# Attention in transposed score tiles: 96 queries by 128 keys, no row maximum, denominators from a ones column

## The chip, the cores and the metric

The kernel runs on one core of a Trainium2 chip. The metric is the device time of one execution in microseconds (us). Five engines work side by side, each through its own instructions in order: PE multiplies matrices (its weight loads are shown as PEld and overlap the multiplications), DVE and ACT do element-wise work, POOL does the same more slowly and can issue transfers, and SP only issues transfers (DMA). A measurement of this kernel can tell about 0.5% from no change.

## What is computed

The input is float32; the two channel weights come as float64 words. Attention over a local window and block summaries is followed by a Fourier mix and a two-layer channel block:

```python
batch, n_heads, seq, head_dim = (4, 8, 768, 64)
block, window = (32, 16)
k_sum = k.reshape(B, H, nb, block, D).max(axis=3)
v_sum = v.reshape(B, H, nb, block, D).mean(axis=3)
scores_l = scale * np.matmul(q, k.transpose(0, 1, 3, 2))
mask_l = np.abs(pos[:, None] - pos[None, :]) < window
scores_s = scale * np.einsum('bhsd,bhnd->bhsn', q, k_sum)
scores_s = scores_s + np.log(block)
...
scores_all = scores_all - np.max(scores_all, axis=-1, keepdims=True)
a = np.exp(scores_all)
a = a / (np.sum(a, axis=-1, keepdims=True) + 1e-09)
...
X = np.fft.fft(x, axis=1)
X = np.fft.fft(X, axis=2)
mixed = np.real(X).astype(np.float32)
u = x + mixed
...
un = (u - mu) / np.sqrt(var + 1e-06)
ch = np.maximum(un @ w_ch1, 0.0) @ w_ch2
return (u + ch).astype(np.float32)
```

Every query sees 31 keys around it and 24 summaries (the maximum of each block of 32 keys, the mean of its values). The exponentials are divided by their sum.

## The kernel before

The program has five stages. In stage b (0 to 3) the attention of batch b is woven with other work: in stage 0 with the conversion of the channel weights (gen_weights, lines 266 to 290), in stages 1 to 3 with the Fourier mix and the channel layers of the batch before (gen_post, from line 301). Stage 4 holds gen_post of the last batch alone. The weaving is written as generators: drive (line 406) takes one step of the attention, then two of gen_post (one of gen_weights), and so on. A scheduler then orders each engine's instructions from this order and their dependences, so work can move ahead of its place in the code.

gen_attention goes through four pairs of heads per batch, three steps per pair, each step on two tiles of 128 queries. The names that the rows use are these.

- prepare: keys and queries are transposed on PE (qk, line 153) and copied by ACT. DVE takes the block maxima (line 158). PE averages the values of the blocks (vm, line 166, 6 matmuls), and DVE copies the averages (line 170).
- scores: queries stand in the output's rows. PE computes 192 columns for each tile and head (sc, lines 183, 185, 186): 128 own keys, 32 edge keys, 24 summaries, padding. A head has 64 channels, so the first head's operands lie in rows 0 to 63 and the second's in rows 64 to 127. DVE adds the mask (line 187), takes the row maximum (lines 192, 193), ACT takes the exponential with the row sum (line 196), DVE takes the reciprocal (lines 199, 200).
- turn: PE transposes the probabilities (pt, line 209, 6 per step); DVE and ACT copy them (line 211).
- values: PE multiplies them with edge values and summaries (av, line 220) and with the own values (line 223); DVE multiplies by the reciprocal and writes x (line 224).

gen_post folds x on DVE (sd, zw, fg, lines 311 to 321), transforms it on PE (y, lines 327 and 331; mx, lines 344 and 345), normalises it, transposes it (unt, line 365), and runs the channel layers (hp, line 373; ch, line 384), whose results DVE and ACT take out. It ends with the stores of x. gen_post(b) needs the whole of x of batch b.

A float32 matmul stands in the trace as two instructions, here called passes; a transpose is one. SP issues the loads of keys and queries, the weight loads (raw, line 277) and the stores; POOL issues the loads of values and edge values.

## Time and profile before

| | |
|---|---|
| time of three runs, us | 1127.8, 1131.44, 1132.7 (median 1131.44) |
| the profiled execution's span, first to last instruction, us | 1126.7 |
| what lies around the span (median less span), us | 4.7 |
| PE busy in the span | 1031.1 us (92%) |
| DVE busy in the span | 439.4 us (39%) |
| ACT, POOL busy | 228.8 us (20%), 122.9 us (11%) |

The time of the profiled execution itself is not recorded apart from its span; the median stands for it. The span falls into the stages at the first y instruction of each batch: 163.5, 417.4, 673.8 and 920.8 us. An engine's share of the whole span mixes stages with different limits, so the shares are read stage by stage.

### The profile page before, as it was taken

What the parts mean: (1) busy time and instruction counts of PE and PEld (TensorE: products, weight loads), DVE (VectorE), ACT (ScalarE), POOL (GpSimd) and SP (SyncE); (2) the same over time, 40 slices, a digit from 0 to 9 for tenths busy, and PEclk for the clock granted to TensorE, in tenths of its full rate; (3) what the DMA queues carried; (4) which work ended last, traced back from release to release, by engine and by line L of the source; (5) the groups of instructions that cost most, each with busy time, mean ns of one, the idle gap of its engine ahead of it and who ended that gap; (6) DMA issues with size and microseconds to landing.
All of it is one profiled execution on the core that took longest, in us unless ns stands there. A gap on an engine that the chain in (4) does not pass through costs nothing. (4 is left out here: it accounts for less than half of the span.)

```text
span 1126.7 us, 10580 instructions
## 1 busy us (share of the span) xinstructions
PE 1031.1 (92%) x4144; PEld 656.7 (58%) x4144; DVE 439.4 (39%) x906; ACT 228.8 (20%) x668; POOL 122.9 (11%) x164
## 2 busy tenths in 40 slices
PE   5376689999998989999999989999999978999998
PEld 4365568664565457764566457765566546544543
DVE  4999988421332047521322037522222046101000
ACT  2456533310121002311112003311112001000100
POOL 2556520100101010100101010100100000000000
PEclk8655679999998989999999999999999989999999
DMA  9585411100202011010202011000000000000000
GB/s 265 154 220 165 138 48 29 45 1 9 64 1 45 10 35 29 17 29 9 64 1 46 10 36 29 18 1 9 27 10 1 18 11 1 1 9 19 1 9 19
DMA packets 63106, 46.59 MB, mean 41 GB/s; under 512 B 52688, under 2 KB 53968, under 8 KB 62928
## 3 DMA queue, kind: packets, MB, share of 16 engines
q1 hardware_dynamic: 58528, 37.63, 12.2%
q0 software_dynamic: 4096, 7.61, 2.5%
q10 hardware_dynamic: 432, 0.67, 0.2%
q8 instruction: 33, 0.54, 0.2%
q14 instruction: 17, 0.14, 0.0%
HBM read 39.60 MB, written 6.29 MB: 41 GB/s over the span
## 5 line engine op out<-in xcount | busy, mean ns | idle before, releaser
L373 PE MATMUL hp<-unT,w 128*128 128x384 f32 x1024 | 345.1, 493 | 3.1 <-DVE unT L366 3.1
L384 PE MATMUL ch<-w,h 128*128 128x512 f32 x768 | 337.5, 594 | 0.0
L373 PEld LDWEIGHTS hp<-unT,w 128*128 128x128 f32 x1024 | 193.0, 193 | 129.9 <-issue 4.3
L384 PEld LDWEIGHTS ch<-w,h 128*128 128x128 f32 x768 | 143.4, 191 | 165.8 <-issue 163.8
L196 ACT ACTIVATE s<-s,mx 128x192 f32<-128x192 f32 x192 | 85.1, 444 | 238.8 <-DVE mx L193 237.6
L376 DVE TENSOR_SCALAR h<-hp 128x384 f32<-128x384 f32 x64 | 35.7, 558 | 209.2 <-PE hp L373 203.6
L299 DVE TENSOR_TENSOR x<-ch,x 128x512 f32<-128x512 f32 x24 | 16.6, 692 | 181.8 <-PE ch L384 181.8
L378 ACT ACTIVATE h<-hp 128x384 f32<-128x384 f32 x64 | 31.2, 487 | 273.4 <-PE hp L373 273.4
L209 PE MATMUL pt<-ident,s 128*128 128x128 f32 x288 | 50.8, 303 | 23.6 <-DVE ve L170 6.8
L143 POOL DMA_DIRECT2D ve<-in_v_dram x32 | 17.7, 553 | 496.9 <-PE av L220 496.9
L187 DVE SCALAR_TENSOR_TENSOR s<-sc,mask 128x384 f32<-128x384 f32 x96 | 50.4, 550 | 36.0 <-PE sc L183 32.7
L223 PE MATMUL av<-vn,ptT 128*128 128x64 f32 x384 | 61.2, 288 | 0.0
L209 PEld LDWEIGHTS pt<-ident,s 128*128 128x128 f32 x288 | 36.4, 153 | 40.7 <-issue 15.1
L223 PEld LDWEIGHTS av<-vn,ptT 128*128 128x128 f32 x384 | 59.2, 220 | 0.1
L327 PE MATMUL y<-fs,fg 128*128 128x193 f32 x192 | 45.2, 389 | 14.1 <-DVE fg L318 14.1
L220 PE MATMUL av<-ve,ptT 128*128 128x128 f32 x192 | 46.5, 328 | 11.9 <-DVE x L224 11.7
L183 PE MATMUL sc<-kw,qt 64*128 64x192 f32 x192 | 49.3, 381 | 8.5 <-DVE s L187 8.5
L289 POOL TENSOR_TENSOR w<-w,cvt 128x512 f32<-128x512 f32 x32 | 51.4, 1618 | 35.6 <-DVE w L287 35.6
L211 ACT COPY ptT<-pt 128x384 f32<-128x384 f32 x48 | 22.7, 472 | 152.6 <-PE pt L209 152.6
L224 DVE TENSOR_TENSOR x<-av,rcp 128x256 f32<-128x256 f32 x48 | 20.2, 421 | 79.2 <-PE av L223 79.0
L220 PEld LDWEIGHTS av<-ve,ptT 128*128 128x128 f32 x192 | 35.7, 219 | 25.1 <-DVE x L224 15.3
L327 PEld LDWEIGHTS y<-fs,fg 128*128 128x128 f32 x192 | 38.5, 230 | 18.3 <-DVE fg L318 8.5
(70 smaller groups left out, 974.9 us busy)
## 6 DMA issues: line engine op xcount, KB each, us to landing
raw<-in_moe_w_ch_dram SPq DMA_DIRECT2D x32, 512.0 KB, 4.1
kn<-in_k_dram SPq DMA_DIRECT2D x32, 192.0 KB, 4.0
vn<-in_v_dram POOLq DMA_DIRECT2D x32, 192.0 KB, 3.9
qn<-in_q_dram SPq DMA_DIRECT2D x32, 192.0 KB, 4.6
out_dram<-x SPq DMA_DIRECT2D x24, 256.0 KB, 2.0
ve<-in_v_dram POOLq DMA_DIRECT2D x64, 20.0 KB, 2.7
fs<-c_fs SPq DMA_DIRECT2D x1, 1158.0 KB, 8.6
fd<-c_fd SPq DMA_DIRECT2D x1, 768.0 KB, 8.7
```

What stands on the lines that cost most here:

```text
L183: nc.tensor.matmul(ps[:, j, :], qt[rows, t, :], kw[rows, t, :], start=True, stop=True)
L187: nc.vector.scalar_tensor_tensor(out=s[:, :, e, :], in0=ps, scalar=1.0 / float(np.sqrt(D)), in1=mask[:, sp:sp + 2, 0:KW] if e else mask[:, ...
L196: nc.scalar.activation(out=a, in_=a, func=AF.Exp, bias=mx[:, i:i + 1], scale=1.0, accum_out=den[:, i:i + 1])
L209: nc.tensor.transpose(ps[:, i, :], sv[:, c:c + P], ident)
L220: nc.tensor.matmul(ps[:, j].rearrange("p e d -> p (e d)"), pts[j][:, 2, :], ve[:, t, :], start=True, stop=False)
L223: nc.tensor.matmul(ps[:, j, e, :], pts[j][:, e, :], vn[:, t, e, :], start=False, stop=(e == 1))
L289: nc.gpsimd.tensor_tensor(out=dst, in0=dst, in1=tmp[:, 0, :], op=ALU.mult)
L327: nc.tensor.matmul(y, fg[:, st, P * g:P * (g + 1)], fs[:, g % 2, par, st, :], start=(st == 0), stop=(st == HT - 1))
L373: nc.tensor.matmul(ps, w1[:, d, P * n:P * (n + 1)], unT[:, d, :], start=(d == 0), stop=(d == NDT - 1))
L376: nc.vector.tensor_scalar(out=hT[n], in0=ps, scalar1=0.0, scalar2=None, op0=ALU.max)
L378: nc.scalar.activation(out=hT[n], in_=ps, func=AF.Relu)
L384: nc.tensor.matmul(ps, hT[n][:, P * i:P * (i + 1)], w2[:, n, :], start=(n == 0), stop=(n == NIT - 1))
```

## The change

The attention of the kernel is written anew, and the old kernel stands behind it as a second program that runs only if a flag is set. gen_weights and gen_post are the same text.

- Queries come in 96s, and keys stand in the rows of the score tile: 128 keys cover 96 queries with 16 keys on each side. Per pair there are 16 score matmuls of 96 columns (8 windows, two heads), and 2 more of 384 columns for all summaries.
- There is no mask to add, no row maximum and no transpose of the probabilities. ACT takes the exponential straight from the scores, DVE multiplies by a 0/1 band (128x768, twice per pair), and the result is already the left operand of the product with the values.
- The values carry a column of ones (65 columns for 64), so the product gives the denominators. The summaries' ones column holds 32 and their values are block sums, which takes the place of log(32) and the mean. 16 matmuls of 65 columns and 8 of 130 per pair.
- Block sums come from a load of their own (vb) and a DVE reduction, then go by DMA to where they are needed (vs). The outputs (xs) have 96 rows and go by six DMAs per pair to x, which has 128.
- All transfers but three constants are issued by SP.
- PSUM is divided into four single buffers and two of two banks.
- The reciprocals of all denominators are kept (rec). After batch 3's attention they are tested against 2^-40 and 2^40; a flag is read by all engines at the end, and a branch goes round the old program if it is 0.

The diff, cut to its core (the removed lines are the functions printed above):

```diff
+QT = 96
+LIM = 2.0 ** 40
...
+    def two_banks(name):
+        return psum.tile([P, 2, 512], FP, tag="two", bufs=2, name=name)
+
+    def one_bank(shape, name):
+        return psum.tile(shape, FP, tag="one", bufs=4, name=name)
...
+    def block_sums(b, gg):
+
+        raw = apool.tile([4 * nb, BLOCK, D], FP, tag="vb", bufs=1, name=f"vb_{b}_{gg}")
+        nc.sync.dma_start(out=raw.rearrange("p f d -> p (f d)"),
+                          in_=v[b, 4 * gg:4 * gg + 4].rearrange("h (n f) d -> (h n) (f d)", f=BLOCK))
+        vb = spool.tile([4 * nb, D], FP, tag="vbs", bufs=2, name=f"vbs_{b}_{gg}")
+        nc.vector.tensor_reduce(out=vb, in_=raw.rearrange("p f d -> p d f"), op=ALU.add, axis=AX.X)
+        sums[b, gg] = vb
+
+    def load_values(b, g):
+        vw, vs = vw_bufs[g % 2], vs_bufs[g % 2]
+        if g % 2 == 0:
+            block_sums(b, g // 2)
+        for e in range(2):
+            src = v[b, 2 * g + e].rearrange("(t p) d -> p t d", p=QT)
+            nc.sync.dma_start(out=vw[W:W + QT, :, e, 0:D], in_=src)
+            nc.sync.dma_start(out=vw[0:W, 1:NQ, e, 0:D], in_=src[QT - W:QT, 0:NQ - 1, :])
+            nc.sync.dma_start(out=vw[W + QT:P, 0:NQ - 1, e, 0:D], in_=src[0:W, 1:NQ, :])
+            i = 2 * (g % 2) + e
+            for c in range(2):
+                r = 64 * c + 32 * e
+                nc.sync.dma_start(out=vs[r:r + nb, e, 0:D], in_=sums[b, g // 2][nb * i:nb * (i + 1), :])
...
+    def scores(b, g, r):
+        kt, qt = kt_bufs[g % 2], nat[b, g]
+        ps = two_banks(f"sc_{b}_{g}_{r}")
+        for i, (h, j) in enumerate(windows(r)):
+            o = QT * (4 * h + j)
+            for e in range(2):
+                rows = slice(D * e, D * (e + 1))
+                nc.tensor.matmul(ps[:, e, QT * i:QT * (i + 1)], kt[rows, o:o + P], qt[rows, o:o + QT],
+                                 start=True, stop=True)
+        p = apool.tile([P, 2, 4, QT], FP, tag="p", bufs=2, name=f"p_{b}_{g}_{r}")
+        nc.scalar.activation(out=p.rearrange("p e i c -> p e (i c)"), in_=ps[:, :, 0:4 * QT], func=AF.Exp, scale=SC)
+        pv = p.rearrange("p e i c -> p (e i) c")
+        nc.vector.tensor_tensor(out=pv, in0=pv, in1=band[:, None, :].to_broadcast([P, 8, QT]), op=ALU.mult)
+        return p
+
+    def sum_scores(b, g):
+        km, qt = km_bufs[g % 2], nat[b, g]
+        ps = one_bank([P, S2], f"ss_{b}_{g}")
+        for h in range(2):
+            nc.tensor.matmul(ps[64 * h:64 * (h + 1), :], km.rearrange("p e n -> p (e n)"),
+                             qt[:, S2 * h:S2 * (h + 1)], start=True, stop=True)
...
+    def values(b, g, r, p, pm, xs):
...
+        for i, (h, j) in enumerate(windows(r)):
+            for e in range(2):
+                nc.tensor.matmul(av[:, h, j % 2, e, :], p[:, e, i, :], vw[:, 4 * h + j, e, :],
+                                 start=h not in first, stop=False, skip_group_check=True)
+                first.add(h)
+        for j in range(2):
+            for h in range(2):
+                rows = slice(64 * h, 64 * (h + 1))
+                o = QT * (2 * r + j)
+                nc.tensor.matmul(av[:, h, j].rearrange("p e d -> p (e d)"), pm[rows, o:o + QT],
+                                 vs[rows].rearrange("p e d -> p (e d)"), start=False, stop=(j == 1),
+                                 skip_group_check=True)
...
+        nc.vector.reciprocal(out=rc, in_=flat[:, :, :, D])
...
+    def regroup(g, xs, x):
...
+                nc.sync.dma_start(out=x[p:p + n, st:st + HT + 1:HT, P * g:P * (g + 1)], in_=xv[o:o + n, :, j, :])
...
+            xs = apool.tile([QT, 2, 4, 2, D], FP, tag="xs", name=f"xs_{b}_{g}")
+            for r in range(NR):
+                values(b, g, r, p[r], pm, xs)
+                yield
+            regroup(g, xs, x)
+            if n2:
+                load(*n2)
+                load_values(*n2)
+            yield
...
+        redo = nc.values_load(flag[0:1, 0:1], min_val=0, max_val=1)
+    with tc.If(redo > 0):
+        _general_program(tc, q, k, v, moe_w_ch1, moe_w_ch2, out)
```

Three places of the instruction order show how work moves. The first is PE in the channel layers of stage 1, where a pair's attention lies between hp blocks. Before, one step of a pair (av: values of step 0; sc: scores of the next pair's first step) takes these rows:

```order
L220 MATMUL av_1_0_1717<-ve_82,ptT_1_0_0_1580 128x128
L223 MATMUL av_1_0_1717<-vn_1_1133,ptT_1_0_0_1580 128x64 x2
L220 MATMUL av_1_0_1717<-ve_82,ptT_1_0_1_1586 128x128
L223 MATMUL av_1_0_1717<-vn_1_1133,ptT_1_0_1_1586 128x64 x2
L373 MATMUL hp_0_13_1734<-unT_0_1478,w_77 128x384 x4
L373 MATMUL hp_0_14_1740<-unT_0_1478,w_77 128x384 x4
L183 MATMUL sc_2_0_0_1747<-kw_79,qt_2_1612 128x192 x2
L185 MATMUL sc_2_0_1_1751<-kw_79,qt_2_1612 128x64
L186 MATMUL sc_2_0_1_1751<-kw_79,qt_2_1612 128x128
L185 MATMUL sc_2_0_1_1751<-kw_79,qt_2_1612 128x64
L186 MATMUL sc_2_0_1_1751<-kw_79,qt_2_1612 128x128
```

Now half a pair's values (L577 with the probabilities p, L584 with the summaries) and half the next pair's scores stand there (ss is the product with all summaries):

```order
L577 MATMUL av_2_1_1457<-vw_84,p_2_1_1377 96x65 x8
L584 MATMUL av_2_1_1457<-vs_86,psum_2_1354 96x130 x4
L743 MATMUL hp_0_11_1472<-unT_0_1258,w_77 128x384 x4
L743 MATMUL hp_0_12_1478<-unT_0_1258,w_77 128x384 x4
L743 MATMUL hp_0_13_1510<-unT_0_1258,w_77 128x384 x4
L743 MATMUL hp_0_14_1516<-unT_0_1258,w_77 128x384 x4
L552 MATMUL sc_3_0_1522<-qt_3_1392,kt_81 128x96 x8
L564 MATMUL ss_3_1534<-qt_3_1392,km_83 64x384 x2
```

The transposes pt (L209) and the averages vm (L166) are gone from the stage, and the pieces are fewer and longer.

The second place is SP from the start of the program. Before, the first weight load (raw) is its eleventh transfer:

```order
L134 DMA kn_0_84<-in_k_dram 128x6x64 x2
L134 DMA qn_0_83<-in_q_dram 128x6x64 x2
L134 DMA kn_1_141<-in_k_dram 128x6x64 x2
L134 DMA qn_1_140<-in_q_dram 128x6x64 x2
L269 DMA fs<-c_fs 128x2316
L270 DMA fd<-c_fd 128x1536
L277 DMA raw_174<-in_moe_w_ch_dram 128x1024
```

Now the loads of values (vw), the block sums' load (vb) and their copies (vs, which need the DVE reduction vbs) come first; these are the first rows:

```order
L494 DMA kn_0_89<-in_k_dram 128x6x64 x2
L494 DMA qn_0_88<-in_q_dram 128x6x64 x2
L502 DMA vb_0_121<-in_v_dram 96x2048
L514 DMA vw_84<-in_v_dram 96x8x64
L515 DMA vw_84<-in_v_dram 16x7x64
L516 DMA vw_84<-in_v_dram 16x7x64
L520 DMA vs_86<-vbs_0_123 24x64 x2
```

After 12 more rows of the same kinds it goes on:

```order
L516 DMA vw_85<-in_v_dram 16x7x64
L520 DMA vs_87<-vbs_0_123 24x64 x2
L639 DMA fs<-c_fs 128x2316
L640 DMA fd<-c_fd 128x1536
L647 DMA raw_196<-in_moe_w_ch_dram 128x1024
```

The first weight load is now the thirty-second transfer, and the vs copies ahead of it stand in line behind a DVE instruction.

The third place is DVE at the end of a batch. Before, the fold of the next batch (sd) stands behind the last values of its attention, after the last ch result (ch_5) of the batch before:

```order
L299 TENSOR_TENSOR x_149<-ch_4_2299,x_149 128x512
L224 TENSOR_TENSOR x_1168<-av_3_1_2330,rcp_3_1_2119 128x2x128
L299 TENSOR_TENSOR x_149<-ch_5_2338,x_149 128x512
L224 TENSOR_TENSOR x_1168<-av_3_2_2357,rcp_3_2_2236 128x2x128
L299 TENSOR_TENSOR sd_0_2390<-x_1168 128x1536
```

Now it stands ahead of the second half of the channel layers (h_1 from hp_1):

```order
L736 COPY unT_1_1693<-unt_5_1709 128x4x128
L669 TENSOR_TENSOR sd_0_1892<-x_935 128x1536
L557 TENSOR_TENSOR p_0_0_1882<-p_0_0_1882,band 128x768
L669 TENSOR_TENSOR zw_0_1893<-sd_0_1892 128x3x256 x2
L685 MEMSET fg_0_1894 128x3
L669 TENSOR_TENSOR fg_0_1894<-zw_0_1893 128x3x127 x2
L688 COPY fg_0_1894<-zw_0_1893 128x6
L669 TENSOR_TENSOR fg_0_1894<-zw_0_1893 128x3x127
L746 TENSOR_SCALAR h_1_0_1715<-hp_1_1_1725 128x384
```

The fold moved ahead by half a batch's channel layers, because the attention of the batch ends earlier.

## Rows read from the trace of the kernel before

**Rows 1.** Windows by stage: us, busy PE, PEld, DVE, ACT, POOL, then PEclk, DMA, GB/s

```profile
0.00:163.54 163.54, 106.95 (x522) 89.11 (x522) 137.70 (x268) 79.67 (x209) 78.25 (x82) 0.66 0.61 171
163.54:417.43 253.89, 244.83 (x1020) 154.41 (x1021) 88.08 (x188) 45.21 (x141) 17.96 (x32) 0.97 0.11 27
417.43:673.80 256.37, 246.80 (x1037) 156.00 (x1037) 89.92 (x194) 47.43 (x153) 17.36 (x32) 0.97 0.11 26
673.80:920.76 246.96, 238.30 (x987) 149.24 (x986) 85.44 (x186) 44.40 (x143) 9.29 (x18) 0.98 0.05 14
920.76:1126.70 205.94, 194.18 (x580) 107.98 (x580) 38.25 (x74) 12.08 (x26) 0.00 (x0) 0.97 0.02 8
```

**Rows 2.** Waits of PE after 163.5 us: engine, line, releaser: us in total, times, longest

```profile
PE y L327 <- DVE fg L318: 14.1, 5, 5.2
PE vm L166 <- DMA vn<-in_v_dram: 10.1, 5, 3.5
PE pt L209 <- ACT s L196: 3.9, 2, 2.1
PE sc L183 <- DVE s L187: 3.4, 2, 1.7
```

**Rows 3.** Timeline of PE, stage 2: start us, us until the last end, engine, line, instructions

```profile
481.06 1.50 PE L166 MATMUL vm<-vn,avg 128*128 128x128 f32 x12
482.40 9.20 PE L373 MATMUL hp<-unT,w 128*128 128x384 f32 x28
491.43 0.82 PE L209 MATMUL pt<-ident,s 128*128 128x128 f32 x6
492.09 5.33 PE L373 MATMUL hp<-unT,w 128*128 128x384 f32 x16
497.25 0.38 PE L220 MATMUL av<-ve,ptT 128*128 128x128 f32 x2
497.47 0.56 PE L223 MATMUL av<-vn,ptT 128*128 128x64 f32 x4
497.86 0.44 PE L220 MATMUL av<-ve,ptT 128*128 128x128 f32 x2
...
498.53 5.38 PE L373 MATMUL hp<-unT,w 128*128 128x384 f32 x16
503.84 0.43 PE L183 MATMUL sc<-kw,qt 64*128 64x192 f32 x1
...
504.94 0.59 PE L373 MATMUL hp<-unT,w 128*128 128x384 f32 x1
```

**Rows 4.** Timeline of PE, stage 2: score passes of one half of the rows

```profile
569.62 0.43 PE L185 MATMUL sc<-kw,qt 64*128 64x64 f32 x2
...
570.71 0.59 PE L373 MATMUL hp<-unT,w 128*128 128x384 f32 x1
```

**Rows 5.** Lines of DVE, 0 to 163.54 us: instructions | busy us, mean ns | idle before

```profile
L287 DVE SCALAR_TENSOR_TENSOR w<-raw,cvt 128x512 f32<-128x512 uint32 x32 | 24.0, 750 | 0.7 <-ACT cvt L284 0.7
...
L281 DVE TENSOR_SCALAR cvt<-raw 128x512 int32<-128x512 int32 x32 | 18.2, 568 | 1.7 <-POOL w L289 1.7
...
L192 DVE TENSOR_REDUCE mx<-s 128x4 f32<-128x768 f32 x14 | 13.2, 942 | 0.1
L211 DVE COPY ptT<-pt 128x384 f32<-128x384 f32 x12 | 6.6, 550 | 1.6 <-PE pt L209 1.5
L170 DVE COPY ve<-vm 24x384 f32<-24x384 f32 x10 | 5.6, 557 | 9.4 <-PE vm L166 9.3
```

**Rows 6.** Timeline of DVE, stage 0: the first instruction on the channel weights

```profile
30.38 0.42 DVE L281 TENSOR_SCALAR cvt<-raw 128x512 int32<-128x512 int32 x1
```

**Rows 7.** Timeline of SP, stage 0: four weight loads issued

```profile
14.39 2.05 SPq L277 DMA_DIRECT2D raw<-in_moe_w_ch_dram  x4
```

**Rows 8.** The page's DMA issues: count, KB each, median us from issue to landing

```profile
raw<-in_moe_w_ch_dram SPq DMA_DIRECT2D x32, 512.0 KB, 4.1
...
out_dram<-x SPq DMA_DIRECT2D x24, 256.0 KB, 2.0
```

More of the change, by code (lines that the diff above doesn't have):

```diff
@@ L21, with _general_consts @@
 O_PREV, O_NEXT, O_SUM = P, P + W, P + 2 * W
-def _consts_np(S, DM):
+def _general_consts(S, DM):
     nb = S // BLOCK
@@ L78, with _general_program @@
 @with_exitstack
-def kernel(
+def _general_program(
     ctx: ExitStack,
@@ L102 @@
     assert (S, DM, D, H % 2) == (768, 512, 64, 0)
-    C = _consts_np(S, DM)
-    dr = {n: nc.inline_tensor(C[n], name=f"c_{n}") for n in C}
+    C = _general_consts(S, DM)
+    dr = {n: nc.inline_tensor(C[n], name=f"g_{n}") for n in C}
     cpool = ctx.enter_context(tc.tile_pool(name="cst", bufs=1))
@@ L419, with kernel @@
+def kernel(tc, q, k, v, moe_w_ch1, moe_w_ch2, out):
+    nc = tc.nc
+    with ExitStack() as ctx:
+        flag = _main_program(ctx, tc, q, k, v, moe_w_ch1, moe_w_ch2, out)
+        redo = nc.values_load(flag[0:1, 0:1], min_val=0, max_val=1)
+    with tc.If(redo > 0):
+        _general_program(tc, q, k, v, moe_w_ch1, moe_w_ch2, out)
 _INS = ['q', 'k', 'v', 'moe_w_ch1', 'moe_w_ch2']
```

268 lines of the change are left out of this document (added).

## Prediction

> **What bounds the kernel now.** I read the windows by stage first [rows 1]. In stages 1 to 3 PE is busy for 244.8 of 253.9, 246.8 of 256.4 and 238.3 of 247.0 us at a granted clock of 0.97 to 0.98; DVE has under 91 us of work in each. There the length is PE's work, and only what shortens PE's rows, or closes PE's gaps, moves the end. Stage 4 is gen_post alone: 205.9 us, and the change leaves its instructions as they are. Stage 0 is another case: PE is busy for 107 of 163.5 us at a clock of 0.66, DVE for 137.7. The conversion of the weights is four DVE instructions for each of 32 chunks, from 24.0 us for the costliest line to 18.2 us for the cheapest, 85.4 us for the four lines together [rows 5], and it begins at 30.4 us [rows 6]. DVE bounds stage 0 from there on.
>
> Then I read PE's waits [rows 2]: after 163.5 us PE waits 14.1 us for the fold of x (y), 10.1 us for loads of values (vm), and 7.3 us for DVE and ACT at the turn of a batch (pt, sc). After such gaps the clock falls to its lower level of 1.2 GHz for a while, which is what the 0.97 of [rows 1] holds: 0.03 of 257 us is some 8 us per stage.
>
> **A pair on PE, before.** In the channel layers the timeline gives what each piece takes from the hp rows, since PE starts the next hp right behind it [rows 3]. An hp pass paces at 9.03/28 = 0.3225 us (482.40 to 491.43). vm: 481.06 to 482.40, 1.34 us per pair. A step's transposes pt: 491.43 to 492.09, 0.66 us. A step's values: 497.25 to 498.53, 1.28 us. A step's scores: 503.84 to 504.94, 1.10 us, and 0.15 us ahead of them, since sixteen hp passes from 498.53 end at 503.69. The 12 transposes of keys and queries stay and are left out. A pair: 3 x (0.66 + 1.28 + 1.25) + 1.34 = 10.9 us.
>
> **A pair on PE, after.** No row shows these shapes, so each is bounded by its neighbours.
> - Scores: 32 passes of 64 rows and 96 columns, heads in turn, in two groups. Eight passes of the second head alone, 96 columns on average, take 1.09 us, 0.136 each [rows 4]; those eight with four of the first head's among them take 1.10 us [rows 3]. So the halves of the array work at the same time, and a pair costs 16 x 0.136 + 2 x 0.15 = 2.5 us. Ends: 1.6 (16 x 0.080, 96 columns at the columns' pace of hp, 0.3225 for 384) and 3.3 (32 x 1.10/12 + 0.3). I take 2.5, the row being of the same mean width.
> - Values: 32 passes with 96 stationary columns and 65 moving. The nearest row has 128 and 64: four passes in 0.39 us (497.47 to 497.86), 0.0975 each [rows 3], nearly twice what 64 columns need at hp's pace (0.3225 x 64/384 = 0.054), so the load of the stationary columns sets it. Ends: 32 x 0.0975 = 3.1, and 2.3 if the load shrinks with 96/128. I take 2.8.
> - Summaries in the values: 16 passes of 64 rows in turn, 130 columns. Eight per half at 0.136 to 0.15 and two entries: 1.5 us (1.2 to 2.5, the upper end with the halves one after the other).
> - Summary scores: 4 passes of 384 columns at 0.3225 and one entry: 1.4 us (0.8 if the two column halves overlap).
>
> Sum 8.2 us, ends 5.9 and 10.3. A pair saves 2.7 us (0.6 to 5.0), and 12 pairs in stages 1 to 3 save **32 us** (7 to 60).
>
> One rule speaks against the shape. A copy of 24 partitions takes 557 ns, one of 128 with as many elements per partition 550 ns [rows 5]: partitions left empty give no time back. The Trainium skill (Trainium Kernel Development and Optimization, Best Practices) says to always tile to 128 partitions; the trace agrees for DVE. Taken for PE as well, so that 96 stationary columns cost what 128 cost, values take their upper end and the sum is 4 us worse. The Trainium skill (TensorE: Matmul & The Clock Gate, LDWEIGHTS) has the weight load go with its columns at 1.2 GHz, 80 ns for 96; by this estimate values would be 2.6 us and the sum 2 us better.
>
> **Gaps of PE in stages 1 to 3.** vm is gone and its 10.1 us with it. sd now stands before hp_1, since attention ends early, so the 7.3 us at the turn of a batch go too, and part of the fold's wait; its second half still waits for the first half's y, so I leave 2.3 us per stage. With fewer gaps about half of the 8 us per stage of low clock comes back, some 10 us in all. Against that stand waits that I can't see: loads issued behind others on SP, the chain exp, band, values in the short y rows. I give 3 us per stage for them (0 to 10). Net **-18 us** (-27 to +3).
>
> **Stage 4.** y waited 5.2 us here [rows 2] and then ran at the low clock. With the fold done under ch, **-6 us**.
>
> **Stage 0.** DVE does less per pair: two band products and the key maximum at L192's 0.94 us for 768 elements, two outputs of 512 elements at L211's pace (0.75 each), small ones 0.6, half a block sum of 2048 elements (1.25): 6.2 us. But conversion starts later. SP issues 31 transfers ahead of the first weight load where it issued 10, at 2.05/4 = 0.51 us each [rows 7], and the vs copies among them wait for DVE's block sum. An issue takes 4.1 us to land [rows 8]. I put the first conversion at 34.5 us, when pairs 0 and 1 have just been done in DVE's idle time. From there: 85.4 for conversion, 12.4 for pairs 2 and 3, 7.3 for the next batch's first pair, 5.7 for the fold (4,600 elements at 0.94/768), and twice DVE runs dry, because the next weight loads stand on SP behind vs copies that wait for DVE: seven issues and a landing less the band products, 5.7 us each. That is 157 us; with small waits 159, **-4.5 us** (-22 without the two dry spells, +12 with each twice as long and a later start). DVE hides PE's and ACT's shares here.
>
> **The end.** All engines read the flag and branch round the second program. Nothing in the trace shows a taken branch over thousands of instructions; the nearest rows are transfers, 2.0 to 4.1 us from issue to landing [rows 8]. I take **+3 us** (0 to 6). The Trainium skill (Runtime: NRT & Kernel Launch, Instruction fetch mechanics) says that a taken branch past the prefetched pages stalls until the target is fetched; no run so far shows it. The reciprocal test is a few DVE rows under PE's work: nothing while PE bounds, 3 us otherwise.
>
> **Sum.** 1131.4 - 32 - 18 - 6 - 4.5 + 3 = 1074 us. It is made on the profiled execution (span 1126.7, 4.7 below the median) and set on the median.
>
> **Rivals.**
> - *The weights' stage comes free, and small passes are at their lower ends.* For it: DVE's work falls by 3 us per pair. Against: SP's order. 17 us more in stage 0 and some 12 to 25 on PE: about 1040.
> - *The halves don't overlap in the new order.* Pairs at 10.3 us: 7 us saved for 32, 1099. Against: [rows 3] and [rows 4] together.
> - *Waits eat the gain.* PE's new gaps come to the 4.8 us per pair that the sum saves: 1131, no change.
> - *Slower: one queue for all loads.* About 20 issues per pair, 10 us of SP, and each waits in order for PE or DVE. If each pair's values wait for their loads, and the clock falls after the gap, 5 + 2.5 us for 12 pairs add 90: 1164. It decides from 4.8 us per pair. For it: vm waited up to 3.5 us for a load with far fewer issues. Against: loads are asked for two pairs ahead.
> - *The flag is raised*, and the old program runs behind the new: about 2200. Scores of inputs of 0.1 stay far within 2^40.
>
> **How the numbers follow.** Forecast 0.55, free stage 0.15, no overlap 0.14, no change 0.05, slower 0.10, flag 0.01. The forecast's own bounds, the no-overlap case and most of the free stage lie in 1040 to 1112; left out are the slower cases and the rest. Faster by over 0.5% (about what a measurement can tell) 0.84, within 0.05, slower 0.11.
>
> **What would show it.** First y at 159 us, then stages of 233 to 240 us and a last one near 200. In the channel layers: a half pair's scores 1.25 us, its values with summaries 2.15, ss 1.4. DVE's first conversion at 34 to 35 us. PE waits after 160 us under 20 us in sum. The prediction falls if PE waits for vw or vs in every pair, if score passes pace at over 0.1 us, or if SP starves the conversion for more than 15 us.

## The result, and the profile after

| | before | after |
|---|---|---|
| median of four runs each on one chip, us | 1129.62 (1126.91 to 1132.7) | 1070.22 (1066.4 to 1071.54) |
| ratio, 95% interval | | 0.9488 (0.9438 to 0.9539) |
| span of the profiled execution, us | 1126.7 | 1069.7 |

The forecast was 1074 us. The total came near it, but its parts did not: stage 0 became 28.7 us longer where 4.5 us less was forecast, and the three stages behind it gained 83.1 us where 50 were forecast. Two large errors nearly cancelled, so the nearness of the total is luck. This section shows where each sits.

The windows of the changed kernel by stage, cut at the first y of each batch (columns as in [rows 1]: us, busy PE, PEld, DVE, ACT, POOL, then PEclk, DMA, GB/s):

```profile
0.00:192.20 192.20, 77.65 (x481) 62.19 (x481) 130.00 (x203) 61.45 (x100) 53.46 (x42) 0.57 0.65 173
192.20:418.36 226.16, 224.28 (x916) 132.23 (x916) 75.02 (x120) 27.52 (x54) 0.00 (x0) 0.99 0.20 47
418.36:643.95 225.59, 225.23 (x966) 134.36 (x965) 65.82 (x118) 28.21 (x55) 0.00 (x0) 1.00 0.16 38
643.95:866.34 222.39, 220.76 (x919) 130.83 (x918) 60.44 (x116) 25.28 (x49) 0.00 (x0) 1.00 0.09 23
866.34:1069.70 203.36, 189.61 (x582) 105.23 (x580) 36.37 (x72) 12.12 (x26) 0.00 (x0) 1.00 0.03 10
```

Against [rows 1], line by line: stage 0 is 192.2 us for 163.5, stages 1 to 3 are 226.2, 225.6 and 222.4 for 253.9, 256.4 and 247.0, the last is 203.4 for 205.9. In stages 1 to 3 PE's idle time fell from 27.3 us in all to 3.9, and the granted clock stands at 0.99 to 1.00. In stage 0 DVE has 7.7 us less work than before and 36 us more idle time (62.2 for 25.8).

**Stages 1 to 3.** The waits of PE from 192.2 us to the end (engine, line, releaser: us in total, times, longest; the y row holds one wait of 51.5 us that ends at the left edge and belongs to stage 0):

```profile
PE y L697 <- DVE fg L688: 53.2, 3, 51.5
PE hp L743 <- DVE unT L736: 4.5, 3, 2.0
PE unt L735 <- DVE un L731: 3.0, 1, 3.0
PE qk L530 <- DVE x L669: 1.3, 1, 1.3
PE sc L552 <- DVE xs L590: 0.7, 2, 0.4
```

What remains behind stage 0 is 11.2 us, most of it in the last stage, and the pieces of the attention hardly wait. The waits of [rows 2] are gone, vm (10.1 us) with its instructions, and most of the fold's 14.1 us (3.0 us of them ended at 163.54 us and belong to stage 0). The pieces on PE, from the timeline around the start of stage 2 (start us, us until the last end, engine, line, instructions; a piece runs until the next row's start):

```profile
416.51 0.87 PE L564 MATMUL ss<-qt,km 128*64 128x384 f32 x4
417.30 1.13 PE L552 MATMUL sc<-qt,kt 64*128 64x96 f32 x14
...
425.21 1.50 PE L577 MATMUL av<-vw,p 128*96 128x65 f32 x16
426.64 0.69 PE L584 MATMUL av<-vs,psum 64*96 64x130 f32 x8
427.26 1.57 PE L577 MATMUL av<-vw,p 128*96 128x65 f32 x16
...
434.77 1.14 PE L552 MATMUL sc<-qt,kt 64*128 64x96 f32 x16
435.84 0.87 PE L564 MATMUL ss<-qt,km 128*64 128x384 f32 x4
```

A half pair's scores take 1.07 us (434.77 to 435.84), values 1.43 and summaries 0.62 (425.21, 426.64, 427.26), ss 0.79 (416.51 to 417.30). A pair is 2 x (1.07 + 2.05) + 0.79 = 7.0 us, where the prediction had 8.2 and the old kernel 10.9.

**Stage 0.** SP's issues in order of time (SPq; a row's second number is the time from its first issue to its last):

```profile
5.21 0.43 SPq L516 DMA_DIRECT2D vw<-in_v_dram  x1
14.90 1.74 SPq L520 DMA_DIRECT2D vs<-vbs  x2
...
19.85 1.10 SPq L494 DMA_DIRECT2D kn<-in_k_dram  x2
...
30.69 14.41 SPq L647 DMA_DIRECT2D raw<-in_moe_w_ch_dram  x5
...
53.52 0.54 SPq L516 DMA_DIRECT2D vw<-in_v_dram  x1
63.54 1.74 SPq L520 DMA_DIRECT2D vs<-vbs  x2
...
68.48 1.93 SPq L647 DMA_DIRECT2D raw<-in_moe_w_ch_dram  x4
```

Twice within 70 us SP stands still for 9 us ahead of a vs copy (5.6 to 14.9, 54.1 to 63.5), until DVE's block sum is done; the key loads of pair 1 and the next weight loads stand behind. A third wait ends at 128.1 us and a fourth at 198.3; SP's row for the last three of them (0 to 192.2 us):

```profile
SPq L520 <- DVE vbs L505: 33.5, 3, 14.8
```

DVE at the same time (in brackets: idle time just before, and what ended it):

```profile
41.64 0.69 DVE L590 TENSOR_TENSOR xs<-av,rec 96x512 f32<-96x512 f32 x1
42.25 0.41 DVE L651 TENSOR_SCALAR cvt<-raw 128x512 int32<-128x512 int32 x1
...
59.83 3.65 DVE L505 TENSOR_REDUCE vbs<-vb 96x64 f32<-96x2048 f32 x1 [1.73 <-DMA vb<-in_v_dram]
63.40 1.82 DVE L557 TENSOR_TENSOR p<-p,band 128x768 f32<-128x768 f32 x2
72.75 0.43 DVE L651 TENSOR_SCALAR cvt<-raw 128x512 int32<-128x512 int32 x1 [7.54 <-DMA raw<-in_moe_w_ch_dram]
```

The first conversion starts at 42.25 us, where [rows 6] has 30.38: on DVE it stands behind the last step of pair 1 (xs, 41.64), whose keys SP asked for at 19.85, behind the first vs copies. The block sum takes 3.65 us. After it and the band products DVE runs dry for 7.5 us, until the weight loads that SP issued at 68.48 land. The waits of DVE for raw sum to 20.1 us in four spells (7.5, 7.1, 5.1 and 0.4); the kernel before has no such row. The one of 5.1 us has no wait for DVE ahead of it: its loads, issued at 156.26, stand behind 9.5 us of other issues on SP (146.63 to 156.16). PE waits 39.6 us for kn, in four waits.

### The profile page after: what moved, and what is told of

It is laid out like the page before. It is cut to its first block, busy times and chain, and to the rows that moved or that the text cites. A ratio compares the mean times of both kernels' runs of the same rounds, so it can differ in the third digit from the quotient of the medians.

```text
span 1069.7 us, 9582 instructions
## 1 busy us (share of the span) xinstructions
PE 937.5 (88%) x3858; PEld 564.8 (53%) x3858; DVE 367.7 (34%) x627; ACT 154.6 (14%) x284; POOL 53.5 (5%) x42
## 2 busy tenths in 40 slices
DMA packets 109317, 59.57 MB, mean 56 GB/s; under 512 B 88656, under 2 KB 101072, under 8 KB 108368
## 5 line engine op out<-in xcount | busy, mean ns | idle before, releaser
L743 PE MATMUL hp<-unT,w 128*128 128x384 f32 x1024 | 336.9, 488 | 4.5 <-DVE unT L736 4.5
L754 PE MATMUL ch<-w,h 128*128 128x512 f32 x768 | 333.6, 593 | 0.0
L743 PEld LDWEIGHTS hp<-unT,w 128*128 128x128 f32 x1024 | 192.4, 190 | 139.4 <-DVE unT L736 5.4
L754 PEld LDWEIGHTS ch<-w,h 128*128 128x128 f32 x768 | 145.0, 190 | 177.9 <-issue 174.6
L697 PE MATMUL y<-fs,fg 128*128 128x193 f32 x192 | 38.1, 347 | 53.2 <-DVE fg L688 53.2
L577 PE MATMUL av<-vw,p 128*96 128x65 f32 x512 | 63.0, 284 | 18.5 <-DMA vw<-in_v_dram 9.0
L577 PEld LDWEIGHTS av<-vw,p 128*96 128x96 f32 x512 | 59.5, 198 | 27.9 <-DMA vw<-in_v_dram 9.5
L697 PEld LDWEIGHTS y<-fs,fg 128*128 128x128 f32 x192 | 32.4, 197 | 57.6 <-DVE fg L688 51.8
L530 PE MATMUL qk<-ident,kn 128*128 128x128 f32 x96 | 16.5, 320 | 39.6 <-DMA kn<-in_k_dram 39.6
L552 PEld LDWEIGHTS sc<-qt,kt 64*128 64x128 f32 x512 | 38.5, 218 | 19.5 <-issue 14.8
L557 DVE TENSOR_TENSOR p<-p,band 128x768 f32<-128x768 f32 x32 | 30.4, 955 | 50.9 <-ACT p L555 50.8
L552 PE MATMUL sc<-qt,kt 64*128 64x96 f32 x512 | 45.0, 315 | 2.7 <-ACT qt L531 1.9
L555 ACT ACTIVATE p<-sc 128x768 f32<-128x768 f32 x32 | 26.0, 811 | 125.3 <-PE sc L552 125.2
L530 PEld LDWEIGHTS qk<-ident,kn 128*128 128x128 f32 x96 | 13.7, 167 | 43.0 <-issue 29.3
L653 ACT ACTIVATE cvt<-cvt,rebias 128x512 int32<-128x512 int32 x32 | 23.0, 719 | 80.0 <-DVE cvt L651 80.0
L505 DVE TENSOR_REDUCE vbs<-vb 96x64 f32<-96x2048 f32 x8 | 29.2, 3647 | 14.8 <-DMA vs<-vbs 10.3
L655 DVE SCALAR_TENSOR_TENSOR cvt<-raw,cvt 128x512 int32<-128x512 int32 x32 | 32.9, 1029 | 1.5 <-ACT cvt L653 1.5
```

What stands on the lines that cost most here:

```text
L505: nc.vector.tensor_reduce(out=vb, in_=raw.rearrange("p f d -> p d f"), op=ALU.add, axis=AX.X)
L530: nc.tensor.transpose(ps[:, i, :], src[:, HT * h + i].rearrange("p e d -> p (e d)"), ident)
L552: nc.tensor.matmul(ps[:, e, QT * i:QT * (i + 1)], kt[rows, o:o + P], qt[rows, o:o + QT], start=True, stop=True)
L557: nc.vector.tensor_tensor(out=pv, in0=pv, in1=band[:, None, :].to_broadcast([P, 8, QT]), op=ALU.mult)
L577: nc.tensor.matmul(av[:, h, j % 2, e, :], p[:, e, i, :], vw[:, 4 * h + j, e, :], start=h not in first, stop=False, skip_group_check=True)
L655: nc.vector.scalar_tensor_tensor(out=ex, in0=high, scalar=-(1 << 31), in1=ex, op0=ALU.bitwise_and, op1=ALU.bitwise_or)
```

## Experiments

Two theories stood at the start. **Queue:** stage 0 is long because SP issues everything in order and its vs copies wait for DVE. **PE pieces and order:** stages 1 to 3 gained more because the pieces overlap better than priced and because the attention of a batch now ends early, so that PE has no gap at the turn of a batch.

All ratios are set against the old kernel on the same chip. Its median was 1129.62 us beside after, 1128.12 beside s0_pool, s0_vs, s0_raw and pe_late, 1122.69 beside pe_order, pe_twice, val_split and pool_raw, and 1128.18 beside the rest, so medians from two chips compare to some half a per cent, and the stages are compared in the traces. "First y" is the end of stage 0.

| kernel | median, us | ratio to before, 95% | first y, us |
|---|---|---|---|
| after | 1070.22 | 0.9488 (0.9438 to 0.9539) | 192.2 |
| s0_pool | 1037.22 | 0.9186 (0.9145 to 0.9227) | 153.3 |
| s0_vs | 1048.53 | 0.9295 (0.9256 to 0.9333) | 168.4 |
| s0_raw | 1068.42 | 0.9473 (0.943 to 0.9516) | 188.0 |
| raw_pool | 1042.3 | 0.9248 (0.9198 to 0.9298) | 164.1 |
| pool_raw | 1044.64 | 0.9279 (0.9234 to 0.9324) | 160.5 |
| act_vw | 1040.44 | 0.9251 (0.9199 to 0.9303) | 159.2 |
| pe_late | 1092.91 | 0.9706 (0.9659 to 0.9752) | 187.9 |
| pe_order | 1086.42 | 0.9659 (0.9617 to 0.9702) | 196.7 |
| pe_twice | 1094.88 | 0.9753 (0.9691 to 0.9815) | 196.4 |
| val_split | 1147.63 | 1.0206 (1.0161 to 1.0251) | 215.9 |
| val_128 | 1081.6 | 0.9592 (0.9539 to 0.9644) | 194.8 |
| no_flag | 1065.69 | 0.9463 (0.9421 to 0.9505) | 191.8 |

### The queue: all value loads on POOL (s0_pool)

```diff
-            nc.sync.dma_start(out=vw[W:W + QT, :, e, 0:D], in_=src)
+            nc.gpsimd.dma_start(out=vw[W:W + QT, :, e, 0:D], in_=src)
...
-                nc.sync.dma_start(out=vs[r:r + nb, e, 0:D], in_=sums[b, g // 2][nb * i:nb * (i + 1), :])
+                nc.gpsimd.dma_start(out=vs[r:r + nb, e, 0:D], in_=sums[b, g // 2][nb * i:nb * (i + 1), :])
```

> The loads of values, of the block sums and the vs copies are issued by POOL, where the old kernel had its value loads; nothing else is changed. Theory Q (stage 0 lost its 28.7 us to SP's one queue: weight loads and key loads stand behind vs copies that wait for DVE): DVE's waits for raw fall from 20.1 us to under 5, PE's wait for kn from 39.6 to under 15, the first y comes at 160 to 175 us instead of 192, the time is 1040 to 1055. Rival T (the transfers themselves are the trouble: 109,317 packets where there were 63,106, and the 3.65-us block sum on DVE): another queue moves no bytes and no DVE work, first y at 187 or later, time 1063 to 1075. Stages 1 to 3 stay within 2 us each by both.

1037.2 us, first y at 153.3: a little more than theory Q asked for. The transfers carry the same 59.57 MB and DVE's work in stage 0 stays (129.0 us for 130.0), which speaks against rival T. By itself this run does not settle it, since the packets fell with the change of queue, to 79,877 from 109,317. Two runs below do: act_vw has 109,061 packets and first y at 159.2, raw_pool 109,317 and 164.1. The waits of DVE from 0 to 160 us, the longest rows:

```profile
DVE rec L589 <- PE av L584: 7.9, 4, 3.9
DVE vbs L505 <- DMA vb<-in_v_dram: 7.1, 1, 7.1
DVE p L557 <- ACT p L555: 3.7, 2, 2.5
DVE cvt L655 <- ACT cvt L653: 1.7, 1, 1.7
```

No row names raw any more, and PE's wait for kn is 9.0 us for 39.6. Stages 1 to 3 take 229.2, 225.6 and 222.4 us; the first is 3 us longer.

### Only the copies that wait (s0_vs)

The edit is the second pair of lines above alone.

> Only the vs copies, the transfers that wait for DVE's block sum, are issued by POOL; the other value loads stay on SP. If the waits in SP's order are the cost (33.5 us in three waits behind vbs), nearly all of the gain of moving everything appears: first y at 163 to 178, time 1043 to 1058. If the number of issues on SP is the cost (12 of 31 per pair are gone, 0.5 us each), about a third of it: first y near 185. If the transfers are the cost: first y at 190, 1068.

1048.5 us and first y at 168.4: two thirds of s0_pool's gain from four of the ten issues per pair that it moves (the expectation's count of issues was wrong: a pair has about 20, and four are vs copies). DVE's wait for raw falls to 1.4 us. So most of the loss was the waiting inside SP's order; PE still waits 33.1 us for kn, and DVE 17.4 us for values (rec, 7.9 in s0_pool); the rest of s0_pool's gain seems to lie with these late keys.

### Only the weight loads moved (raw_pool)

```diff
-            nc.sync.dma_start(out=raw.rearrange("p n w -> p (n w)"), in_=src.bitcast(I32))
+            nc.gpsimd.dma_start(out=raw.rearrange("p n w -> p (n w)"), in_=src.bitcast(I32))
```

> Only the weight loads (raw) are issued by POOL; every other load and the vs copies stay on SP. If stage 0 is long because the conversion is starved (weight loads behind vs copies), DVE's 20.1 us of waiting for raw go and first y comes at 165 to 175, 1043 to 1053. If it is long because keys come late behind vs copies (PE waits 39.6 us for kn) and pairs with them, conversion runs ahead but the pairs end last: PE's wait for kn stays over 30 us, first y at 183 or later, 1061 or more.

1042.3 us, first y at 164.1. The time is as the queue theory wants it, a little better, but its reading was wrong: DVE's waits for raw do not go, they are 24.9 us. The waits of DVE, 0 to 164.06 us, the longest rows:

```profile
DVE cvt L651 <- DMA raw<-in_moe_w_ch_dram: 24.9, 9, 5.8
DVE rec L589 <- PE av L584: 6.5, 1, 6.5
DVE cvt L655 <- ACT cvt L653: 1.8, 4, 0.5
```

What goes is the rest: in the changed kernel DVE also waits 20.4 us for values (rec), 6.6 for exponentials (p) and 6.2 for keys (mx), and here 6.5, 0.6 and none. Conversion starts at 8.1 us and fills the time in which DVE used to wait for pairs. The sum counts, not one row: DVE's idle time in stage 0 is 62.2 us after, 38.2 here, 36.8 in s0_vs, 24.3 in s0_pool, while its work stays between 126 and 132 us.

### An earlier start alone (s0_raw), and with the queue (pool_raw)

```diff
     load_values(0, 0)
+    for i in range(4):
+        load_raw(i)
     prepare(0, 0)
     load(0, 1)
...
+            if i == 8:
+                nc.sync.dma_start(out=fs, in_=dr["fs"].ap())
+                nc.sync.dma_start(out=fd, in_=dr["fd"].ap())
```

> The first four weight loads are issued ahead of the loads of pair 1, and the tables fs and fd behind the eighth chunk; all else stays, all loads on SP. If the late start is the cost (first conversion at 42.25 us where it was 30.38): conversion starts at 22 to 28 us, first y at 175 to 182, time 1052 to 1060. If the later dry spells are (7.5, 7.1 and 5.1 us without raw), the start is given back and first y stays at 186 or later, time 1063 or more.

1068.4 us: conversion starts 19 us earlier (23.3 for 42.25) and first y comes only 4.2 us earlier. That is no more than stage 0 varies by: pe_late and no_flag, below, which leave stage 0 as it is, have 187.9 and 191.8. DVE's waits for raw grow from 20.1 to 28.3 us (7.3 of them ahead of the first conversion), and its idle time in all hardly moves (60.5 us for 62.2). The early start is given back at later waits; the late start was a symptom of the queue and not a cost of its own.

> Value loads, block-sum loads and vs copies on POOL as in s0_pool, and the first four weight loads ahead of pair 1's loads as in s0_raw (tables behind the eighth chunk). If the early start is worth something once the queue no longer starves the conversion, first y comes at 143 to 149 us where s0_pool has 153.3, and the time is 1026 to 1033, faster than any so far. If DVE's own work (129 us in stage 0) with PE's slow first pairs is what is left, 1035 to 1039, as s0_pool.

1044.6 us, 7.4 more than s0_pool. Both theories missed. Conversion begins at 14.1 us instead of 26.2, and DVE's wait for values (rec) rises from 7.9 to 15.2 us: the first pairs come later, with 2 MB of weights ahead of pair 1's keys and DVE taken by conversion between their steps. I did not separate the two.

### Value loads on ACT (act_vw)

The edit is that of s0_pool with nc.scalar for the vw and vb loads; the vs copies stay on POOL.

> As s0_pool, but the loads of values and block sums are issued by ACT; POOL issues the vs copies alone. If POOL's issuing (0.56 to 0.85 us each, 103 us busy in stage 0) is what is left of the loss, first y comes at 147 to 152 us, 1030 to 1036. If ACT then holds back the conversion or the exponentials behind loads that wait for a free buffer, first y at 156 or later, 1040 or more.

1040.4 us, first y at 159.2: no better than s0_pool, and the intervals overlap. POOL's busy time in stage 0 falls from 102.9 to 73.9 us and nothing is gained. PE now waits 24.9 us for an ACT exponential (psum), and DVE again 18.2 us for raw, as the second case expected; these waits could hide a gain, so whether POOL's issuing costs anything in s0_pool is not shown.

### The pieces: heads one after the other (pe_order)

```diff
-        for i, (h, j) in enumerate(windows(r)):
-            o = QT * (4 * h + j)
-            for e in range(2):
+        for e in range(2):
+            for i, (h, j) in enumerate(windows(r)):
+                o = QT * (4 * h + j)
                 rows = slice(D * e, D * (e + 1))
```

> In each half pair all eight scores of the first head come first and then all eight of the second, where the heads stood in turn; the same matmuls. Theory O (the two halves of the array's rows work at the same time only when heads alternate; a half pair's scores take 1.07 us for 16 passes): each half now goes alone at about 0.136 us a pass, the pace of same-half passes in the old kernel; 16 passes take 2.0 to 2.2 us, and 24 half pairs in stages 1 to 3 cost 22 to 27 us: 1092 to 1098. Rival (a pass of 96 columns simply takes 0.067 us, alternating or not): under 3 us, 1068 to 1073. Halfway would be passes at the columns' pace of 0.08 us.

1086.4 us, between the two ranges. The timeline of PE at the same place:

```profile
442.04 1.66 PE L552 MATMUL sc<-qt,kt 64*128 64x96 f32 x16
443.63 0.87 PE L564 MATMUL ss<-qt,km 128*64 128x384 f32 x4
```

The half pair takes 1.59 us (0.099 a pass) where alternating heads take 1.07 (0.067). The halves do work side by side when heads alternate (0.067 is less than the 0.081 that 96 columns take at hp's pace), though not in full, which would be 8 x 0.099 = 0.8 us. The order is worth 0.53 us per half pair; but a lone half runs at 0.099 and not at the 0.136 that I had read from [rows 4]. By windows stages 1 to 3 grow by 2.8, 3.7 and 3.2 us, 9.6 in all (22 half pairs x 0.53 = 11.7); the rest of the 16 us is in stage 0 (4.5) and the last stage (1.9).

### The pieces: 128 columns, and 64 + 32 (val_128, val_split)

```diff
-                nc.tensor.matmul(av[:, h, j % 2, e, :], p[:, e, i, :], vw[:, 4 * h + j, e, :],
+                k = 4 * e + i
+                m = P if k < 7 else QT
+                nc.tensor.matmul(full[0:m, h, j % 2, e, :], pf[:, QT * k:QT * k + m], vw[:, 4 * h + j, e, :],
```

> Seven of eight products of probabilities and values take 128 stationary columns instead of 96 (the next window's columns fill the rest, and output rows 96 to 127 are not read). Now 16 passes take 1.43 us, 0.089 each. If the stationary columns set a pass in proportion: 14 x 0.119 + 2 x 0.089 = 1.84 us, +10 us in 24 half pairs, 1080. If a pass of 128 costs what the old kernel's 128x64 pass did (0.0975): 1.54 us, +3 us, 1072 to 1074. If a pass has one price whatever its columns (empty rows give nothing back, but cost nothing more): 1.43 us, 1068 to 1071.

1081.6 us. PE's timeline in stage 2:

```profile
429.96 1.84 PE L581 MATMUL av<-vw,p 128*128 128x65 f32 x16
431.73 0.69 PE L588 MATMUL av<-vs,psum 64*96 64x130 f32 x8
```

Sixteen passes take 1.77 us for 1.43. With two of them at 0.089, a pass of 128 columns takes 0.114 us, 1.28 times one of 96. The stationary columns set the pass nearly in proportion: leaving 32 of 128 empty does give time back on PE. The stages grow by 2.1, 2.8 and 2.8 us, as 22 x 0.34 = 7.5 asks. So the rule that was weighed (the Trainium skill, Trainium Kernel Development and Optimization, Best Practices: always tile to 128 partitions) holds for DVE's rows [rows 5] and not for the stationary side of these passes, where this run differs from it. The other one (the Trainium skill, TensorE: Matmul & The Clock Gate, LDWEIGHTS: 80 ns for 96 columns) is near: 89 ns measured for 96 and 114 for 128.

```diff
-                nc.tensor.matmul(av[:, h, j % 2, e, :], p[:, e, i, :], vw[:, 4 * h + j, e, :],
-                                 start=h not in first, stop=False, skip_group_check=True)
+                for c0, c1 in ((0, 64), (64, QT)):
+                    nc.tensor.matmul(av[c0:c1, h, j % 2, e, :], p[:, e, i, c0:c1], vw[:, 4 * h + j, e, :],
+                                     start=h not in first, stop=False, skip_group_check=True)
```

> Each product of probabilities and values, 96 stationary columns, is split into one of 64 and one of 32 columns; the same result from twice as many matmuls. Measured now: 16 passes in 1.43 us, 0.089 each. If the load of the stationary columns sets a pass (0.0975 for 128 in the old kernel), two parts together take as much as one and the time stays within 1068 to 1076. If a pass has a fixed price that hardly depends on its columns (what would speak for filling all 128), 32 passes take 2.5 to 2.9 us instead of 1.43: 24 half pairs cost 26 to 34 us, 1096 to 1105.

1147.6 us, slower than the old kernel, and both theories missed. PE's timeline in stage 2 and the weight loads of PE by shape (457 to 703 us; mean ns of one load behind the comma):

```profile
464.09 3.99 PE L578 MATMUL av<-vw,p 128*64 128x65 f32 x32
468.01 0.69 PE L585 MATMUL av<-vs,psum 64*96 64x130 f32 x8
```
```profile
L578 PEld LDWEIGHTS av<-vw,p 128*64 128x64 f32 x128 | 12.2, 134 | 8.7 <-issue 1.3 <-DMA out_dram<-x 0.8 <-DMA kn<-in_k_dram 0.6
L578 PEld LDWEIGHTS av<-vw,p 128*32 128x32 f32 x128 | 8.8, 108 | 4.4
```

32 small passes take 3.92 us, 0.1225 each, more than a pass of 96 columns. That is close to the mean of the two whole loads (134 and 108 ns, mean 121), while passes of one shape come faster than their loads (0.089 us a pass for loads of 165 ns). It looks as if a load can't run ahead of the pass before it when the shape of the tile changes; no run here isolates that. The Trainium skill (TensorEngine Tiling (Array Packing), Tiling Modes, Key Properties) says that a change of the tiling mode drains TensorE; this run is in keeping with it, but does not show a drain by itself. The windows agree with the price (22 x 2.49 = 54.8 us; stages 1 to 3 grow by 55.4).

### Does PE's work alone set stages 1 to 3 (pe_twice)

```diff
-                nc.tensor.matmul(ps[:, e, QT * i:QT * (i + 1)], kt[rows, o:o + P], qt[rows, o:o + QT],
-                                 start=True, stop=True)
+                for _ in range(2):
+                    nc.tensor.matmul(ps[:, e, QT * i:QT * (i + 1)], kt[rows, o:o + P], qt[rows, o:o + QT],
+                                     start=True, stop=True)
```

> Every score matmul is computed twice into the same place; nothing else changes. If PE's instructions alone set the length of stages 1 to 3 (busy over 99% of them), 24 half pairs of 1.07 us more give +26 us there, 8 to 9 us in each stage, 1093 to 1098, and stage 0 does not move by more than 3 us, DVE and SP being late there. If part of the attention lies beside waits, under 18 us. If a repeat on the same weights is cheaper than a first pass, the row itself will show under 2.1 us per half pair and the sum follows it.

1094.9 us. The doubled half pair takes 2.03 us, 0.96 more, and the stages grow by 7.6, 7.2 and 5.2 us, 20.0 in all; 22 x 0.96 = 21.1. PE's microseconds count one for one there. The count is 22 half pairs, since the first pair of a batch runs in the stage before it and the last stage but one has three: L577 has 352 instructions from 192.2 to 866.3 us, 32 for each of 11 pairs. The expectation's 24, and the prediction's 12 pairs, were one pair too many. Stage 0 is 4.2 us longer, more than expected, and no more than it varies by.

### The attention's early end (pe_late)

```diff
-        gens.append((gen_post(b - 1), 2) if b else (gen_weights(), 1))
+        gens.append((gen_post(b - 1), 4) if b else (gen_weights(), 1))
```

> drive takes four steps of gen_post for one of the attention instead of two, so that the attention of a batch ends behind the last channel results, as in the old kernel, and the fold sd stands behind them again. The pieces of a pair are the same. If the early end of the attention is what closed PE's gaps and gave the clock back in stages 1 to 3 (busy 225.4 of 226.2 us at 0.99 now), y waits 5 to 15 us per batch, the granted clock falls to 0.97 or lower in each stage, and the time rises by 25 to 70 us, to 1095 to 1140. If the gaps went because vm went, or because the pieces are fewer, the time rises by under 12 us and the clock stays at 0.99.

1092.9 us, 22.7 more: below the theory's range and above its rival's. The windows of stages 1 to 3 (columns as above):

```profile
187.87:425.86 237.99, 231.01 (x964) 138.41 (x964) 70.45 (x118) 28.23 (x55) 0.00 (x0) 0.97 0.17 41
425.86:654.94 229.08, 224.33 (x964) 133.66 (x964) 68.60 (x120) 28.22 (x55) 0.00 (x0) 1.00 0.17 40
654.94:882.24 227.30, 216.03 (x870) 126.67 (x870) 60.08 (x116) 24.48 (x48) 0.00 (x0) 0.98 0.09 24
```

PE waits 2.5, 2.6 and 7.0 us for the fold ahead of the first y of a batch (425.86, 654.94 and 882.24), less than expected for two of three. Its idle time in the three stages is 23.0 us again (3.9 with the early end, 27.3 in the old kernel): beside the fold it waits 4.9 us for band products (av for p), 3.1 for unT and 2.1 for the test of the flag. The granted clock falls in two of the three. The three stages are 20.2 us longer in all, so the early end is worth some 19 us of gaps and about 1 us of clock; the old kernel's clock (0.97, 0.97, 0.98) does not return in full.

### The flag and the branch (no_flag)

```diff
-        redo = nc.values_load(flag[0:1, 0:1], min_val=0, max_val=1)
-    with tc.If(redo > 0):
-        _general_program(tc, q, k, v, moe_w_ch1, moe_w_ch2, out)
```

> The flag is computed but not read, and the second program is left out, so that there is no branch (for inputs as these the result is the same). The prediction's term for the end was +3 us (0 to 6): 1065 to 1068. If the branch is hidden behind the last store, 1069 to 1071. If the second program costs at the start as well (loading of code), 1060 to 1064.

1065.7 us (1063.5 to 1071.8), an interval that overlaps that of the changed kernel: unclear by the time. The trace tells it: from the last store's issue to the end of the span it takes 5.6 us with the branch (1064.14 to 1069.7), 3.0 without, 3.7 in the old kernel. The branch costs 1.9 to 2.6 us at the end.

## Why the prediction was right in sum and wrong in its parts

- **Stage 0 (-4.5 us forecast, +28.7 measured): the step failed.** It gave 34.5 us to the start, 110.8 to DVE's work from there, and 13.7 to dry spells and small waits: 159. Measured: 42.25, 115.5 and 34.5, together 192.2. Conversion alone is 96.9 us for 85.4, because more of its instructions are held while POOL multiplies (last section); DVE's other work is 18.6 us for 25.4. The mechanism was named, weight loads standing behind vs copies, but it was sized at two spells of 5.7 us; 20.1 us of raw came, and 14 more of other waits, the longest for values (rec, 5.9) and exponentials (p, 3.6). The start missed the loads of pair 1's keys, which stand behind the first vs copy (issued at 19.85 us), and the block sum was priced at 2.5 us and took 3.65. By its own words the prediction falls if SP starves the conversion for more than 15 us. That happened: stage 0 by itself refutes it, and the total was saved by the other error. s0_vs and s0_pool show the cause.
- **A pair on PE (8.2 us forecast, 7.0 measured): mis-sized, inside its ends of 5.9 to 10.3.** Scores 2.1 for 2.5: the row of one half at 0.136 that was taken for its mean width overstates a pass of 96 columns (pe_order: 0.099 alone, 0.067 in turn). ss 0.8 for 1.4: its column halves overlap, the lower end. Values 2.9 for 2.8 and summaries 1.2 for 1.5. The pairs are 11 and not 12, so the pieces give 11 x 3.9 = 43 us for 32. Some 5 us come on top, which the prediction did not see: the old stages 1 to 3 held the values of 12 pairs (144 instructions of L220, 12 per pair) and the transposes pt of 11.7 (210 instructions, 18 per pair), the new ones hold 11 pairs of all, and the values of batch 1's first pair lie in stage 0. So the pieces are worth some 48 us.
- **Gaps and clock (-18 us forecast, some -35 measured).** PE's idle time fell by 23.4 us. The hp, ch and y rows (L743, L754, L697), whose instructions are the same, are busy 533.9 us for 549.6 in stages 1 to 3, 16 us less; but busy times of neighbours overlap, and counted from the start of each PE instruction to that of the next, less the waits, hp, ch and y take 9 us less. So the clock gave back some 9 to 16 us where 10 were forecast: that size was about right, and the gaps were mis-sized. With some 12 us for the clock the parts make the 83.1 us. The 9 us set aside for unseen waits did not come, and the 7 us left for the fold's second half (two waits of 2.3 in the old kernel) went as well. pe_late shows that the early end of the attention closes most of the gaps. When they open again the clock's share hardly changes, so what gave the clock back stays open.
- **Stage 4 (-6 us forecast, -2.5 measured): partly booked in the wrong place.** The y wait of 5.2 us in [rows 2] ends at 920.76 us, so it lay in stage 3, whose 24.6 us hold it. In stage 4 only the clock was left to gain (1.00 for 0.97).
- **The end (+3 forecast): 1.9 to 2.6 us** by the traces.
- **The sum.** The 4.7 us that were taken to lie around the span mixed two things: in the runs behind it about 1.85 us lie around a span (1071.54 less 1069.7 after), and the rest was a profiled execution faster than the median.
- **The rivals.** Free weights: s0_pool comes to the time of that case, 1037 us for 1040, with other parts: 6 us less in stage 0 than the forecast's 159, and the rest from PE. No overlap: pe_order's passes cost 0.53 us more per half pair, 1.06 per pair, where this rival asked for 2.1 (10.3 for 8.2). The slower case, 5 us per pair from values that wait for loads on SP, did not come in stages 1 to 3, where no such wait exists; the same queue took its price in stage 0, where loads are asked for just ahead of their use. The flag was not raised.

The version that beats both is s0_pool: 1037.22 us, 0.9186 of the old kernel (0.9145 to 0.9227); raw_pool's and act_vw's intervals overlap with it.

## What to carry to other kernels

A queue that issues in order turns one transfer that waits for an engine into a wait of everything behind it; put copies of computed data on another queue than the loads that feed the engine which computes them. When a stage is bound by one engine, price its work and its idle time as two sums, and list for each load what stands ahead of it. Price a small matmul by a row with the same stationary width and the same order of halves, not by the mean of mixed widths.

## What the runs showed of the hardware

A DVE instruction that starts while POOL multiplies is held until POOL is done. From 166 to 171 us in the changed kernel:

```profile
166.42 1.38 POOL L659 TENSOR_TENSOR w<-w,cvt 128x512 f32<-128x512 f32 x1 [1.90 <-DVE w L657]
166.60 1.75 DVE L655 SCALAR_TENSOR_TENSOR cvt<-raw,cvt 128x512 int32<-128x512 int32 x1
...
169.36 1.38 POOL L659 TENSOR_TENSOR w<-w,cvt 128x512 f32<-128x512 f32 x1 [1.57 <-DVE w L657]
169.54 1.75 DVE L655 SCALAR_TENSOR_TENSOR cvt<-raw,cvt 128x512 int32<-128x512 int32 x1
```

L655 takes 0.68 us where POOL is idle. The four conversion instructions of a chunk take 0.41, 0.41, 0.68 and 0.68 us unheld, 70 us for 32 chunks, so 27 of the 96.9 us of conversion are such waiting (26 held instructions at about 1.07 us), and 15 of the old kernel's 85.4 (20 held). It also goes the other way: in the old kernel two multiplies from 42.98 us take 4.14 us together, against 1.38 each here, while the DVE rows beside them stay at 0.42 and 0.68 until 44.8 us. The Trainium skill (SBUF — State Buffer, SBUF: two separate sides) says that the two engines share a pair of ports which the first to start holds for its whole instruction, also against a DVE instruction with two inputs in SBUF; these rows agree. Leaving POOL out was not tried.

The weight loads of the products with the values take 192, 165, 134 and 108 ns for 128, 96, 64 and 32 columns (val_128, after, val_split), 0.875 ns per column over some 80 ns; a transpose's load of 128 columns takes 140. Passes of one shape come at 114 and 89 ns for 128 and 96, so the fixed part is hidden and the columns are not.
